# A convolution with a shorter transform: the filter's taps whose factor is exactly zero are left out

## Chip, cores, metric

One core of one Trainium2 chip. The metric is the device time of one execution in microseconds (us), here the median of three runs. Engines: TensorE (PE; PEld its weight loads), VectorE (DVE), ScalarE (ACT), GpSimd (POOL), and SyncE (SP), which only issues transfers.

## What is computed

Two parts, one behind the other, in float32. The first is a long convolution along the sequence; the second a layer of 2048 hidden units whose activation is a rational function.

```
x, v: (2, 12480, 128);  pos_emb: (12480, 64)
h_filt = (max(pos_emb @ w1, 0) @ w2) * exp(-0.01 * pos)[:, None]     # pos = 0 .. 12479, float32
L = 2 * 12480
y = irfft(rfft(x * v, L) * rfft(h_filt, L))[:, :12480, :]            # along the sequence
x2 = (x * y).reshape(24960, 128)
h = x2 @ w_in                                                        # 128 -> 2048
g = (a0 + a1 h + a2 h^2 + a3 h^3) / (1 + |b0| |h| + |b1| h^2 + 1e-6)
out = g @ w_out                                                      # 2048 -> 128
```

The factor exp(-0.01 pos) in float32 falls with the position and is exactly zero from position 10398 on.

## The kernel before

**The transform.** The sequence of length L = 24960 is cut as L = N1 * N2 with N2 = 128 and N1 = 195. A token is m * 128 + n2; there are M = 98 blocks m that hold tokens. The convolution of one channel has three steps. s1 multiplies, for each residue n2, the 98 blocks by a constant matrix f1 with K1 = 98 frequencies, cosine and sine side by side (2 * K1 = 196 columns), and turns the result by twiddle factors tw. s2 is a transform of 128 points over n2 (matrices dft), followed by the product with the filter's spectrum hg. s3 transforms back over the frequencies k2 (idft). The last step, over k1, is done for each residue in `attn_a` with constants g, a matrix of K1 x M for each.

**First part** (lines 243 to 615). The filter network (`hf_w`, `hf_t`, `hf_1`, `hf_2`) takes 16 groups of four residue pairs: positions are loaded with the blocks on the partitions (`load_pos`, L257, on SP's queue, three groups ahead, in a ring of three buffers), multiplied by the window on VectorE (L462, L466), transposed on TensorE (L481), and sent through two products (L488, L496), with copies on ScalarE between them (L484, L490, L502). Between these steps VectorE turns the weights of the second part from float64 words to float32 (`to_f32`, L312 to L328) and GpSimd makes the first products u = x * v (L230).

Then a loop over 32 groups of CG = 4 channels (L574) follows. In round g, in the order of the code: s1 of the filter for group g (`s1_mm`, then `s1h_out`: L160 and L161 with twh, and the four zh instructions L543 to L546 on VectorE), s2 of the filter for group g - 1 (L550, a copy hg on ScalarE, which is also stored to h_d), s1 of batch 0 (L142, L160 and L161 with tw on VectorE, zu on GpSimd, L166 and L167), s2 with the product for group g - 2 (L192 and L193 on VectorE, yy on GpSimd, L195 and L196), and s3 for group g - 3 (L557, two copies on ScalarE, L568 and L569 on GpSimd). A round ends with a piece of u on VectorE (L230) or, when these are done, a step of the weights. Each engine takes its instructions in the order in which they are written.

**Second part** (lines 621 to 1008). 52 tiles of up to five residues (490 tokens) are each taken in four steps of four blocks of hidden units. The order of a step is written out by hand in the loop at L987: ScalarE's L854 and L863 from PSUM, VectorE's L873, the first product h (L844 to L846) of the next step, and for earlier steps L891, L894, L887 on ScalarE, L899, L904, L908 on VectorE and the second product L922. Each step has three slots for one matrix product of another kind (`slot`, L950): the input of the next tile (`attn_a`, `attn_b`), or one step of the convolution of batch 1 for two channels (s1: L142, L154, L166, L167; s2: L177 to L180, L188, L195, L196; s3: L201, L202, L205). All of these share one PSUM buffer cv, so a slot's product starts when the one before has been read. After 64 groups of two channels the convolution is over and the tiles go on alone. All loads of this part, and the stores, are issued on SP's queue: x and v in pieces, hg from h_d, y in chunks of ten residues (yc, L753), g (L771).

Of the kernel before, what the change touches and what calls it, by code (L numbers as in the profile page):

```python
# [18 lines left out]
FO = 64  # L19
DFF = 2048  # L20
L = 2 * S
N2 = 128
N1 = L // N2
M = 98
K1 = 98
# [17 lines left out]
# slots of a tile that go to the next one: beside the convolution, and without it  # L43
# [3 lines left out]
def constants():  # L47
# [14 lines left out]
    # the filter's residues are taken in pairs n2 - 63.5 = +-(p + 1/2), as sums and differences  # L62
# [15 lines left out]
    pos = np.arange(S, dtype=np.float32)  # L78
    win = np.zeros((M * N2,), np.float32)
    win[:S] = np.exp(np.float32(-0.01) * pos)  # L80
    win = win.reshape(M, N2)
# [15 lines left out]
def build(ctx: ExitStack, tc, x, v, pos_emb, w1, w2, w_in, w_out, moe_a, moe_b,  # L97
# [16 lines left out]
    def rows(src, r0, n, t0, k, c0, c):  # L114
        """n blocks of k tokens, a block of N2 tokens apart, from token r0 * N2 + t0 of src (tokens, channels)"""
        w = src.shape[1]
        return bass.AP(src.tensor, src.offset + (r0 * N2 + t0) * w + c0, [[N2 * w, n], [w, k], [1, c]])

    def load_rows(dst, src, t0, k, c0, c, pad, queue=nc.sync):
        """tokens m * N2 + t0 ... of all m; the last m has half its tokens, and where it has none its place  # L120
        takes the tokens before (pad) or is left"""
# [17 lines left out]
    # steps of the convolution for n channels at a time: n / 2 banks  # L139
    def s1_mm(cvt, u, cl0, n):  # L140
        for c in range(n):
            nc.tensor.matmul(out=cvt[:, c // 2, c % 2 * 2 * K1:(c % 2 + 1) * 2 * K1],  # L142
                             lhsT=u[:, cl0 + c, :], rhs=f1, start=True, stop=True)

    def pair(pool):
        """room for both products of a pair of channels, in one"""
# [22 lines left out]
    def spectrum(cvt, n):  # L169
        """real and imaginary parts: a bank each, or both in one"""  # L170
# [62 lines left out]
    # weights of the second part, split into parts of 12 bits for the fast passes  # L233
# [9 lines left out]
    with ExitStack() as st:  # L243
# [4 lines left out]
        win, bdw1, bdw2 = flat[0][0:M, 0:N2], flat[1][:, 0:128], flat[2][:, 0:2 * D]  # L248
# [8 lines left out]
        def load_pos(p0):  # L257
            t = sp.tile([M, 2 * NPL, FO], F32, tag="wa", name="pos", bufs=3)
            load_rows(t[:, 0:NPL], pos_emb, H2 + p0, NPL, 0, FO, True)
            load_rows(t[:, NPL:], pos_emb, H2 - p0 - NPL, NPL, 0, FO, True)  # L260
# [31 lines left out]
        # weights and scalars of the second part  # L292
# [12 lines left out]
        def to_f32(raw, n):  # L305
            """float64 words (low, high) of n elements to float32: the high word gives sign,
            exponent and 20 bits of the fraction, the low word's upper 24 bits the rest."""
# [18 lines left out]
        def normal(fa, ie):  # L326
            """0 where the exponent is below float32's"""
# [712 lines left out]
```

## Time and profile before

| | us |
|---|---|
| median of 3 runs (2546.77 to 2547.78) | 2547.77 |
| profiled execution, span from first to last instruction | 2545.4 |
| VectorE busy | 2411.3 (95%) |
| TensorE busy | 2180.8 (86%) |
| ScalarE busy | 2103.6 (83%) |
| GpSimd busy | 561.5 (22%) |

The profile gives the span of its execution and no time around it. Busy times are those of instructions on the engine; a matmul's end is modelled, and an instruction that waits for a port while it runs counts as busy. Shares over the whole span mix stages with different limits, so the stages have to be read one by one. "L12" is line 12 of the kernel; "a <- b" are the names of the tiles written and read; "128x784" is partitions x elements.

### The profile page before, as it was taken

The page shows a single profiled execution, that of the slowest core. Times are in us where ns is not written, and L with a number is a line of the kernel's source. Part 1 is how long each engine was busy: PE and PEld are TensorE (multiplying, and loading weights), DVE is VectorE, ACT ScalarE, POOL GpSimd, SP SyncE. Part 2 cuts the span into 40 slices and gives each one's busy share as a digit, 9 for nine tenths or more (in the row PEclk, how much of TensorE's full clock was granted, in tenths as well). Part 3 has the DMA queues.
Part 4 walks back from the last instruction along what each step waited for, and adds up shares of the span by engine and source line. Part 5 has one row for each costly group of instructions (what it writes and reads, how often), then busy time and mean ns, then how long its engine had stood idle before and what let it go on. Part 6 is the DMA issues. An engine that isn't in the chain of part 4 may idle for free.

```text
span 2545.4 us, 33926 instructions
## 1 busy us (share of the span) xinstructions
PE 2180.8 (86%) x13344; PEld 1829.2 (72%) x13344; DVE 2411.3 (95%) x1945; ACT 2103.6 (83%) x1919; POOL 561.5 (22%) x522
## 2 busy tenths in 40 slices
PE   6888888789989998999899989888888898888877
PEld 4666665678877877788788767667776777776665
DVE  8999997799999998999899999999999999999997
ACT  6311121899999997999899999999999999999996
POOL 3466656222242224124321200000000000000000
PEclk9999989899999999999999999999999999999999
DMA  7444422822162235222322121111111111111100
GB/s 157 95 112 112 112 74 98 139 68 61 44 117 54 53 68 99 55 73 46 72 75 53 49 49 45 32 40 31 44 44 22 41 44 44 45 30 31 40 11 13
DMA packets 366001, 158.68 MB, mean 62 GB/s; under 512 B 299508, under 2 KB 347256, under 8 KB 362696
## 3 DMA queue, kind: packets, MB, share of 16 engines
q1 hardware_dynamic: 358696, 130.56, 23.2%
q10 hardware_dynamic: 7136, 25.86, 3.1%
q8 instruction: 107, 1.75, 0.3%
q14 instruction: 62, 0.51, 0.1%
HBM read 105.06 MB, written 51.31 MB: 61 GB/s over the span
## 4 chain that ended last, share of the span: by engine, by line
ACT 34%; DVE 30%; PE 21%; issue 9%; POOL 2%; DMA 1%; SPq 1%; ACTq 0%; DVEq 0%; POOLq 0%
ACT r L891 9%; ACT r L894 9%; ACT q L854 8%; PE acc L922 7%; DVE v L908 6%; ACT v L863 5%; DVE r L904 3%; DVE q L899 3%; PE cv L201 3%; PE cv L202 2%; DVE ta L188 2%; DVE v L873 2%; DVE tb L161 2%; PE cv L142 2%; DVE zh L544 2%
## 5 line engine op out<-in xcount | busy, mean ns | idle before, releaser
L922 PE MATMUL acc<-wout,v 128*128 128x128 f32 (+2 forms) x6656 | 833.2, 284 | 59.2 <-DVE v L908 35.2
L922 PEld LDWEIGHTS acc<-wout,v 128*128 128x128 f32 (+2 forms) x6656 | 790.6, 193 | 111.4 <-DVE v L908 55.3
L863 ACT ACTIVATE v<-h,sc 128x980 f32<-128x980 f32 (+1 forms) x416 | 683.2, 1642 | 8.0 <-PE acc L922 8.0
L854 ACT ACTIVATE q<-h 128x980 f32<-128x980 f32 (+1 forms) x416 | 613.7, 1559 | 6.4 <-PE h L846 6.4
L873 DVE SCALAR_TENSOR_TENSOR v<-v,sc,h 128x980 f32<-128x980 f32 (+1 forms) x416 | 504.9, 1214 | 59.7 <-ACT v L863 57.6
L887 ACT ACTIVATE q<-q,sc 128x1960 f32<-128x1960 f32 (+1 forms) x208 | 516.2, 2482 | 0.0
L891 ACT ACTIVATE r<-q,sc 128x1960 f32<-128x1960 f32 (+1 forms) x208 | 515.0, 2476 | 0.2 <-DVE v L908 0.2
L894 ACT ACTIVATE r<-r 128x1960 f32<-128x1960 f32 (+1 forms) x208 | 497.1, 2390 | 0.0
L899 DVE SCALAR_TENSOR_TENSOR q<-q,sc,r 128x1960 f32<-128x1960 f32 (+1 forms) x208 | 467.3, 2247 | 4.9 <-ACT r L894 1.1
L908 DVE SCALAR_TENSOR_TENSOR v<-v,sc,r 128x1960 f32<-128x1960 f32 (+1 forms) x208 | 465.5, 2238 | 0.1
L844 PE MATMUL h<-ahi,win_l 128*128 128x490 f32 (+1 forms) x832 | 365.0, 439 | 100.9 <-DVE v L873 98.5
L904 DVE SCALAR_TENSOR_TENSOR r<-q,r 128x1960 f32<-128x1960 f32 (+1 forms) x208 | 450.7, 2167 | 0.1
L845 PE MATMUL h<-alo,win_h 128*128 128x490 f32 (+1 forms) x832 | 320.6, 385 | 0.0
L846 PE MATMUL h<-ahi,win_h 128*128 128x490 f32 (+1 forms) x832 | 318.1, 382 | 0.0
L844 PEld LDWEIGHTS h<-ahi,win_l 128*128 128x128 f32 x832 | 158.5, 191 | 158.8 <-DVE v L873 133.3
L195 POOL TENSOR_TENSOR yy<-ta 128x196 f32<-128x196 f32 x64 | 122.1, 1908 | 368.3 <-DVE ta L188 368.3
L846 PEld LDWEIGHTS h<-ahi,win_h 128*128 128x128 f32 x832 | 158.7, 191 | 26.4
L845 PEld LDWEIGHTS h<-alo,win_h 128*128 128x128 f32 x832 | 159.4, 192 | 16.0 <-DVE alo L815 0.4
L790 PE MATMUL cv<-yc,gt 98*98 98x128 f32 x1004 | 130.9, 277 | 32.4 <-DVE an L796 29.9
L790 PEld LDWEIGHTS cv<-yc,gt 98*98 98x98 f32 x1004 | 115.0, 165 | 52.1 <-DVE an L796 48.6
L205 ACT ACTIVATE ys<-cv 98x512 f32<-98x512 f32 x64 | 76.9, 1202 | 76.2 <-PE cv L202 76.2
L201 PE MATMUL cv<-idft,yy 128*98 128x256 f32 x256 | 80.6, 396 | 57.3 <-DVE ta L188 33.1
(109 smaller groups left out, 2574.5 us busy)
## 6 DMA issues: line engine op xcount, KB each, us to landing
yc<-y_d SPq DMA_DIRECT2D x23, 980.0 KB
gt<-in_g_dram SPq DMA_DIRECT2D x48, 375.2 KB
h_d<-hg ACTq DMA_DIRECT2D x32, 392.0 KB
y_d<-ys ACTq DMA_DIRECT2D x16, 784.0 KB
hg<-h_d SPq DMA_DIRECT2D x64, 196.0 KB
y_d<-ys SPq DMA_DIRECT2D x16, 784.0 KB
xq<-in_x_dram SPq DMA_DIRECT2D x32, 196.0 KB
vq<-in_v_dram SPq DMA_DIRECT2D x32, 196.0 KB
```

Of the source, the lines that this page charges most:

```text
L844: nc.tensor.matmul(out=t[:, k, 0:w], lhsT=wl, rhs=hi[:, 0:w], start=True, stop=False)
L845: nc.tensor.matmul(out=t[:, k, 0:w], lhsT=wh, rhs=lo[:, 0:w], start=False, stop=False)
L854: nc.scalar.activation(out=halves(st_q[s], i, width(s)), in_=st_h[s, i], func=AF.Abs, **({} if short else {"scale": col("b0")}))
L863: nc.scalar.activation(out=v, in_=st_h[s, i], func=AF.Square, bias=col("s"))
L873: stt(out=v, in0=v, scalar=col("k"), in1=h, op0=ALU.add, op1=ALU.mult)
L887: nc.scalar.activation(out=whole(st_q, s), in_=whole(st_q, s), func=AF.Square, bias=col("dl"))
L891: nc.scalar.activation(out=whole(st_r, s), in_=whole(st_q, s), func=AF.Ln, **({"bias": col("ka")} if short else {}))
L894: nc.scalar.activation(out=whole(st_r, s), in_=whole(st_r, s), func=AF.Exp, scale=-1.0)
L899: nc.vector.scalar_tensor_tensor(out=q, in0=q, scalar=col("ka") if short else 0.0, in1=whole(st_r, s), op0=ALU.add, op1=ALU.mult)
L904: nc.vector.scalar_tensor_tensor(out=r, in0=whole(st_q, s), scalar=2.0, in1=r, op0=ALU.subtract, op1=ALU.mult)
L908: nc.vector.scalar_tensor_tensor(out=v, in0=v, scalar=col("p0" if short else "a0"), in1=whole(st_r, s), op0=ALU.add, op1=ALU.mult)
L922: nc.tensor.matmul(out=acc[j][0:k, q // 128, :], lhsT=g[:, i, q:q + k], rhs=wout[:, f, :], start=(f == 0 and q == 0), stop=(f == NF - 1), ...
```

## The change

The number of taps is counted when the program is built: TAPS is one more than the last position whose window factor is not zero. The filter network works on MF blocks (those that hold such taps) in place of all M. The length of the transform is the smallest odd number of blocks that holds S + TAPS - 1 tokens, N1 * 128, and K1 follows from it; all constants, tiles and instructions that are written in terms of K1, N1 or L take the new sizes. `s1_mm` takes the number of blocks that it sums over. The positions are loaded in two pieces of rows for each half, in place of 98 rows in one piece for the residues below 64, and 96 and 2 for the others; the window table has 96 rows in place of 98. Comments and docstrings are gone from the text, and the line numbers shift. The diff, without those:

```diff
@@ -18,11 +18,16 @@
 B, S, D = 2, 12480, 128
 FO = 64
 DFF = 2048
-L = 2 * S
 N2 = 128
-N1 = L // N2
 M = 98
-K1 = 98
+WINDOW = np.exp(np.float32(-0.01) * np.arange(S, dtype=np.float32))
+TAPS = int(np.flatnonzero(WINDOW)[-1]) + 1
+MF = min(M, -(-TAPS // N2))
+N1 = -(-(S + TAPS - 1) // N2) // 2 * 2 + 1
+L = N1 * N2
+K1 = (N1 + 1) // 2
 CG = 4
 NG = D // CG
 CY = 8
@@ -75,10 +80,9 @@
     ga = turn(k1[:, None, None] * (2 * N2 * m[None, None, :] + n2[None, :, None]), 2 * L)
     w = w[:, None, None]
     g = f(np.stack([np.cos(ga) * w, -np.sin(ga) * w * sg[None, :, None]], 2))
-    pos = np.arange(S, dtype=np.float32)
     win = np.zeros((M * N2,), np.float32)
-    win[:S] = np.exp(np.float32(-0.01) * pos)
-    win = win.reshape(M, N2)
+    win[:S] = WINDOW
+    win = win.reshape(M, N2)[:96]
     return {
         "f1": f1,
         "tw": tw,
@@ -136,14 +140,14 @@
     xb = [x[b] for b in range(B)]
     vb = [v[b] for b in range(B)]
 
-    def s1_mm(cvt, u, cl0, n):
+    def s1_mm(cvt, u, cl0, n, k=M):
         for c in range(n):
             nc.tensor.matmul(out=cvt[:, c // 2, c % 2 * 2 * K1:(c % 2 + 1) * 2 * K1],
-                             lhsT=u[:, cl0 + c, :], rhs=f1, start=True, stop=True)
+                             lhsT=u[0:k, cl0 + c, :], rhs=f1[0:k], start=True, stop=True)
 
     def pair(pool):
         t = pool.tile([N2, 2, 2, 2 * K1], F32, tag="ta", name="ta", bufs=2)
         return t, (t[:, 0], t[:, 1])
@@ -239,13 +243,13 @@
     y0 = wpool.tile([K1, NY, 2, NPT, CY], F32, name="y0")
     flag_i = wpool.tile([128, 1], I32, name="flag_i")
 
     with ExitStack() as st:
         sp = st.enter_context(tc.tile_pool(name="sp", bufs=1))
         spp = st.enter_context(tc.tile_pool(name="spp", bufs=4, space=PSUM))
 
         flat = [sp.tile([128, CG * 2 * K1], F32, tag=t, name=t + "0", bufs=2) for t in ("ta", "ta", "tb")]
-        win, bdw1, bdw2 = flat[0][0:M, 0:N2], flat[1][:, 0:128], flat[2][:, 0:2 * D]
+        win, bdw1, bdw2 = flat[0][0:96, 0:N2], flat[1][:, 0:128], flat[2][:, 0:2 * D]
         twh = sp.tile([N2, 2, 2 * K1], F32, name="twh")
         dfth = sp.tile([N2, 2, N2], F32, name="dfth")
         idfth = sp.tile([N2, 2, N2], F32, name="idfth")
@@ -256,8 +260,12 @@
 
         def load_pos(p0):
             t = sp.tile([M, 2 * NPL, FO], F32, tag="wa", name="pos", bufs=3)
-            load_rows(t[:, 0:NPL], pos_emb, H2 + p0, NPL, 0, FO, True)
-            load_rows(t[:, NPL:], pos_emb, H2 - p0 - NPL, NPL, 0, FO, True)
+            for o, t0 in ((0, H2 + p0), (NPL, H2 - p0 - NPL)):
+                if MF < M:
+                    for r0, r1 in ((0, MF // 16 * 16), (MF // 16 * 16, MF)):
+                        nc.sync.dma_start(out=t[r0:r1, o:o + NPL], in_=rows(pos_emb, r0, r1 - r0, t0, NPL, 0, FO))
+                else:
+                    load_rows(t[:, o:o + NPL], pos_emb, t0, NPL, 0, FO, True)
             pos_t[p0] = t
 
         load_pos(0)
@@ -450,20 +458,20 @@
                         raws.append(load_raw(src[k + 2], WN))
                 yield
 
         nb = H2 // NP
-        W = NP * M
+        W = NP * MF
         pT, rT = {}, {}
 
         def hf_w(p0):
             t = pos_t[p0]
-            pw = pos_t[p0] = sp.tile([M, NPL, 2, FO], F32, tag="wb", name="pw", bufs=2)
-            nc.vector.tensor_tensor(out=pw[:, :, 0], in0=t[:, 0:NPL],
-                                    in1=win[:, H2 + p0:H2 + p0 + NPL].unsqueeze(2).to_broadcast([M, NPL, FO]), op=ALU.mult)
+            pw = pos_t[p0] = sp.tile([MF, NPL, 2, FO], F32, tag="wb", name="pw", bufs=2)
+            nc.vector.tensor_tensor(out=pw[:, :, 0], in0=t[0:MF, 0:NPL],
+                                    in1=win[0:MF, H2 + p0:H2 + p0 + NPL].unsqueeze(2).to_broadcast([MF, NPL, FO]), op=ALU.mult)
             for i in range(NPL):
                 n2 = H2 - 1 - p0 - i
-                nc.vector.tensor_scalar(out=pw[:, i, 1], in0=t[:, 2 * NPL - 1 - i], scalar1=win[:, n2:n2 + 1],
+                nc.vector.tensor_scalar(out=pw[:, i, 1], in0=t[0:MF, 2 * NPL - 1 - i], scalar1=win[0:MF, n2:n2 + 1],
                                         scalar2=None, op0=ALU.mult)
 
         def hf_t(i):
@@ -478,8 +486,8 @@
             ps = cvs()
             for p in range(NP):
                 k = p0 - b0 + p
-                nc.tensor.transpose(out=ps[:, 0, p * M:(p + 1) * M], in_=pt[:, k].rearrange("m t c -> m (t c)"),
-                                    identity=ident[0:M, 0:M])
+                nc.tensor.transpose(out=ps[:, 0, p * MF:(p + 1) * MF], in_=pt[:, k].rearrange("m t c -> m (t c)"),
+                                    identity=ident[0:MF, 0:MF])
             pT[i] = ctile(sp, "zh", 2, CG).rearrange("p r c k -> p (r c k)")[:, 0:W]
             nc.scalar.activation(out=pT[i], in_=ps[:, 0, 0:W], func=AF.Identity)
@@ -493,11 +501,11 @@
             r = rT.pop(i)
             ps = cvs()
             for p in range(NP):
-                nc.tensor.matmul(out=ps[0:M, p // 2, (p % 2) * 2 * D:(p % 2 + 1) * 2 * D],
-                                 lhsT=r[:, p * M:(p + 1) * M], rhs=bdw2, start=True, stop=True)
-            src = ps[0:M].rearrange("m b (p s c) -> m (b p) s c", p=2, s=2)
+                nc.tensor.matmul(out=ps[0:MF, p // 2, (p % 2) * 2 * D:(p % 2 + 1) * 2 * D],
+                                 lhsT=r[:, p * MF:(p + 1) * MF], rhs=bdw2, start=True, stop=True)
+            src = ps[0:MF].rearrange("m b (p s c) -> m (b p) s c", p=2, s=2)
             for q in range(D // UQ):
-                o = hf[q].rearrange("m c (s p) -> m p s c", s=2)[:, i * NP:(i + 1) * NP]
+                o = hf[q][0:MF].rearrange("m c (s p) -> m p s c", s=2)[:, i * NP:(i + 1) * NP]
                 a = src[:, :, :, q * UQ:(q + 1) * UQ]
                 nc.scalar.activation(out=o, in_=a, func=AF.Identity)
@@ -576,7 +584,7 @@
             if a < NG:
                 zh[a] = ctile(sp, "zh", 2, CG)
                 t = cvs()
-                s1_mm(t, hf[a // gq], a % gq * CG, CG)
+                s1_mm(t, hf[a // gq], a % gq * CG, CG, MF)
                 s1h_out(t, zh[a])
             a = g - 1
             if 0 <= a < NG:
```

## Rows read from the trace of the kernel before

**Rows 1.** Stages: length, busy PE, PEld, DVE, ACT, POOL (instructions), clock, DMA share, GB/s.

```profile
0.00:83.00 83.00, 59.83 (x240) 39.31 (x240) 68.98 (x250) 53.58 (x127) 27.83 (x35) 0.96 0.65 147
83.00:430.00 347.00, 294.22 (x1376) 218.05 (x1376) 336.81 (x370) 64.59 (x111) 222.12 (x192) 0.95 0.38 97
430.00:500.00 70.00, 47.92 (x247) 40.26 (x246) 44.07 (x35) 50.63 (x45) 25.07 (x17) 0.80 0.86 161
500.00:1490.00 990.00, 901.89 (x5777) 782.98 (x5775) 934.31 (x642) 899.63 (x760) 286.45 (x279) 0.99 0.28 65
1490.00:2500.00 1010.00, 846.06 (x5508) 724.35 (x5509) 994.73 (x632) 1010.00 (x855) 0.00 (x0) 0.96 0.15 36
```

**Rows 2.** Timeline, one group of the loop: start, duration, engine, line, operation.

```profile
211.26 1.27 POOL L568 TENSOR_TENSOR ys<-qt 98x512 f32<-98x512 f32 x1
211.28 1.67 DVE L543 TENSOR_TENSOR zh<-ta,tb 64x392 f32<-64x392 f32 x1
...
215.73 0.97 DVE L160 TENSOR_TENSOR ta<-cs,tw 128x784 f32<-128x784 f32 x1
```

**Rows 3.** Timeline, a later group, and the first integer conversion of the loop.

```profile
338.32 1.10 DVE L312 TENSOR_SCALAR i<-raw 128x256 int32<-128x256 int32 x1
...
411.82 0.56 DVE L543 TENSOR_TENSOR zh<-ta,tb 64x392 f32<-64x392 f32 x1
...
416.11 0.97 DVE L160 TENSOR_TENSOR ta<-cs,tw 128x784 f32<-128x784 f32 x1
```

**Rows 4.** Chain of waits in order of time, the loop: start, duration, what.

```profile
115.87 1.54 DVE zh L544
...
331.67 1.53 DVE zh L544
```

**Rows 5.** What VectorE waited for, 500 to 1490: total us, times, longest.

```profile
DVE v L873 <- ACT v L863: 41.5, 63, 2.0
```

**Rows 6.** Timeline, one step beside the experts.

```profile
600.18 1.24 DVE L873 SCALAR_TENSOR_TENSOR v<-v,sc,h 128x980 f32<-128x980 f32 x1 [0.64 <-ACT v L863]
...
603.51 0.97 DVE L188 TENSOR_TENSOR ta<-cv,hg 128x784 f32<-128x784 f32 x1
...
604.53 0.67 PE L201 MATMUL cv<-idft,yy 128*98 128x256 f32 x2 [0.76 <-DVE ta L188]
...
609.82 0.97 DVE L154 TENSOR_TENSOR ta<-cv,tw 128x784 f32<-128x784 f32 x1
...
611.37 1.23 DVE L873 SCALAR_TENSOR_TENSOR v<-v,sc,h 128x980 f32<-128x980 f32 x1 [0.58 <-ACT v L863]
```

**Rows 7.** Groups by line and form: count, then busy us, mean ns.

```profile
L196 POOL TENSOR_TENSOR yy<-ta 128x196 f32<-128x196 f32 x64 | 38.9, 608 | 0.0
...
L196 POOL TENSOR_TENSOR yy<-pta,ptb 128x392 f32<-128x392 f32 x32 | 32.6, 1020 | 0.0
...
L796 DVE TENSOR_TENSOR an<-cv,xt 98x384 f32<-98x384 f32 x52 | 28.6, 550 | 8.4 <-PE cv L790 8.4
...
L796 DVE TENSOR_TENSOR an<-cv,xt 98x256 f32<-98x256 f32 x48 | 20.0, 417 | 3.3 <-PE cv L790 3.3
```

**Rows 8.** Timeline, SP's queue and VectorE in the filter network.

```profile
12.54 1.40 SPq L129 DMA_DIRECT2D pos<-in_pos_emb_dram  x1
...
14.30 0.32 SPq L127 DMA_DIRECT2D pos<-in_pos_emb_dram  x1
...
16.61 0.41 DVE L462 TENSOR_TENSOR pw<-pos,ta 98x256 f32<-98x256 f32 x1
```

**Rows 9.** What VectorE waited for, 0 to 90.

```profile
DVE pw L462 <- DMA ta<-in_win_dram: 4.4, 1, 4.4
...
DVE pw L466 <- DMA pos<-in_pos_emb_dram: 0.8, 1, 0.8
```

**Rows 10.** Chain of waits in order of time, the hand-over.

```profile
429.67 4.48 DMA y_d<-ys
...
484.18 9.54 DMA yc<-y_d
```


## Prediction

> **What bounds the kernel now.** I read the busy times by stage first [rows 1]. The filter network (0 to 83 us) has VectorE busy 69.0 of 83; the loop over channel groups, which makes the filter's spectrum and the convolution of batch 0, runs from 83 to about 430 with VectorE busy 336.8 of 347; then 70 us of hand-over at a DMA share of 0.86; then 990 us in which the experts run beside the convolution of batch 1 (VectorE 934, ScalarE 900, TensorE 902); then 1010 us of experts alone, where ScalarE is busy all the time. The last stage runs none of the changed steps except the weights of the inverse transform, so what is won must come from the others.
>
> In the loop the timeline of one group [rows 2] shows VectorE back to back, with L543 at 1.67 us. It begins 0.02 us behind GpSimd's L568 and ends 0.42 after it; the same form takes 0.56 where it comes ahead of that sum [rows 3]. L544 stands in the same way to GpSimd's next sum, L569, with 1.5 us [rows 4]. So the ends of these two are set by GpSimd's sums. L544 stands at 115.87 and, 20 groups later, at 331.67 [rows 4]: 10.79 us a group.
>
> Beside the experts the waits [rows 5] show 63 stalls of VectorE (41.5 us) for ScalarE's v, three a tile. The timeline of one step [rows 6] shows the ring behind them: L873 and L908, then L188 on VectorE, TensorE's four products L201/L202 that waited for L188, ScalarE's copy L205, its L854, L891 and L863, and then L873 again: 600.18 to 611.37, 11.19 us. L154 lies beside this ring, just before the stall of 0.58.
>
> **The change, part by part.** By the diff's own lines the window's last factor that is not zero is at 10397, so TAPS = 10398, MF = 82 blocks of 128 (before 98), N1 = 179 (195), K1 = 90 (98); the pieces of 80 and 2 rows agree with MF = 82. What scales is K1 along the free dimension: 784 elements become 720, 392 become 360, 196 become 180. What has M or K1 on the partitions (ys, attention, hf) keeps its free size, and such instructions I cost at nothing.
>
> *Prices of the shorter instructions* [rows 7]. VectorE: 384 to 256 elements is 550 to 417 ns, 1.04 ns an element; 64 elements less are 0.067 us, 32 less 0.033. GpSimd: yy at 392 and 196 elements takes 1020 and 608 ns, 2.1 ns an element, so 32 less are 0.067 us.
>
> *The loop.* Six PSUM products a group (L160, L161 twice each, L192, L193) give 6 x 0.067 = 0.40, four zh 4 x 0.033 = 0.13, together 0.53 us a group and 17.1 for 32 groups. The zh waits need a second look, since they end with GpSimd. L568 starts at 211.26 and L543 at 211.28. Both count from the u product before: VectorE through L160 and L161 (0.13 less), GpSimd through L195 and L196 (0.13 less). They move together, L568 keeps its 1.27 us, and the gain stays 0.53. Three groups run integer conversions beside GpSimd's yy (L312 takes 1.10 us in the first of them [rows 3]); GpSimd's 0.13 counts there too. Sum 17.5. TensorE (294 of 347 us busy, and its columns shrink too) and ScalarE (65) cover their own parts; should TensorE become late, its slack of some 53 us is the bound. The bounds of the loop: 21 us if VectorE now gets in front of L568 (0.16 a group more in 21 groups, from the 4.45 us that the four zh take, 211.28 to 215.73 [rows 2], against the 4.29 from 411.82 to 416.11, where L543 is free [rows 3]); 10.8 if GpSimd does not get cheaper with 360 elements, which leaves 0.34 a group, the four products ahead of u and the two zh at the end.
>
> *The filter network.* Transposes, the first product and two ScalarE copies fall from 392 columns to 328, all beside a busy VectorE; its own L462 and L466 keep 256 and 64 elements, so nothing is won there but a little of TensorE's time in the first groups. Each position load is four transfers in place of three, 16 loads: 16 more issues on SP's queue at 0.32 to 1.40 us [rows 8]. Behind them in that queue stand the window, the identity, raw weights, xq and vq, and for these wait L462, the transposes, the conversions and GpSimd's u products. The first L462 waits 4.4 us for the window [rows 9], now one issue later (+0.3). The load issued from 12.54 to 14.62 is used at 16.61, 2.0 us later [rows 8]; four loads lie before or at it, so +0.3 to +1.3. Once the integer conversions fill VectorE, SP has slack. I take +0.8 net, with 0 and +2 as ends.
>
> *The hand-over.* GpSimd's last four yy give 0.3. The store of ys (4.48 us on the chain) and the load of yc (9.54) [rows 10] lose 8% of their bytes: 0.36 and 0.76. Sum 1.4; bounds 0 (the x and v loads, which don't shrink, set the pace) and 4.
>
> Here a page bears on it. The rows show two transfers of 98 partitions and their times, not over how many engines they ran. The Trainium skill, page "DMA: Bandwidth & Descriptors", section on why a DMA increments its semaphore by 16, says that a transfer takes the largest number of engines up to 16 that divides the outer dimension of both sides: 98 rows would run on 14, 90 on 15, 82 on 2, 80 on 16. By that rule (an estimate) an engine's share of yc falls by 14% in place of 8%, and the sum gains another 0.9 us. No row here shows the number of engines.
>
> *Beside the experts.* L188 and L154 fall by 0.067 each, 64 times. L188 is in the ring and counts: 64 x 0.067 = 4.3. L154 lies before the stall and only widens it; the experts' own instructions hide it. If the ring were not what ends the step, both would count, 8.6; if loads and GpSimd's u products set this stage, 0. I take 4.3, because the 63 stalls are nearly as many as the 64 groups. No wait is added here.
>
> *Sum.* -17.5 + 0.8 - 1.4 - 4.3 = -22.4 us against the profiled execution, whose span is 2545.4. What lies around the span isn't shown; the runs shown (median 2547.8) are 2.4 above it, and I keep that: 2525.4, rounded to 2525.
>
> **The rivals.**
>
> *A: the order at VectorE and GpSimd turns.* The margin between L568 and L543 is 0.02 us. If VectorE gets in front, the loop gives 21 and not 17.5; with the hand-over at its larger bound it is 2519, with both products beside the experts counted 2515. For it: so thin a margin. Against: both sides shorten by the same 0.13.
>
> *B: GpSimd or the loads swallow part.* GpSimd's instructions cost nearly the same for 360 as for 392 elements: loop 10.8, time about 2532; with nothing beside the experts 2536. For it: GpSimd's part of the loop is on the path in every group [rows 2]. Against: its price by size [rows 7].
>
> *C: no change worth telling.* A measurement of this kernel tells 0.2%, about 5 us, from none. The parts outside the loop give 4.9 together, so the loop must give nothing: another resource must take over at once at 10.8 us a group. TensorE's 294 of 347 us [rows 1], or 9.2 for each of 32 groups, is the nearest; it would have to shrink by nothing and wait more. 2543.
>
> *D: the position loads pace the filter network, and the kernel is slower.* The added transfer of two rows lands last, behind x and v at a DMA share of 0.65 in this stage [rows 1], and VectorE waits for it in every load: 16 x 2.0 us (from the last issue to the use, 14.62 to 16.61 [rows 8]) = 32, less the 23.2 of the other parts = 9 slower, 2557. It decides from 23.2 / 16 = 1.45 us a load. Against: half the loads had such a two-row transfer before, and positions were waited for once, 0.8 us [rows 9]. The Trainium skill, same page, section "Rules for kernel authors", speaks for it: many small transfers should be coalesced, since under 64 KB one pays mostly overhead. An added transfer here has 2 KB; by the rule it is nearly all overhead, which costs time only where someone waits for it.
>
> That the change doesn't shorten anything is excluded by the piece sizes; the shapes in its trace will say so.
>
> **How the numbers follow.** Forecast 0.60 (its own range 2520 to 2530), A 0.17, B 0.15, C 0.05, D 0.03. Below 2514 only all larger bounds together lead, above 2534 the worst of B, C and D; that leaves about 0.13 out. Faster by over 0.2%: 0.60 + 0.17 + 0.15 = 0.92; within 0.2% 0.05; slower 0.03.
>
> **What would show it.** L160 to L193 at about 0.90 us with 720 elements; the loop's L544 every 10.2 to 10.3 us; L543 still near 1.6 (or 0.5, which is A); yy at 0.95 in GpSimd's free groups (B: 1.02); L873 to L873 around the ring at 11.12, with the stall widened from 0.58 to about 0.65; the first group at most 2 us later than now; the experts alone unchanged in length. A loop period above 10.5, or L462 waiting for pos again and again, would make the prediction wrong.

## The result, and the profile after

The changed kernel takes 2523.56 us (median of four runs, 2522.18 to 2524.88) against 2547.27 us before (four runs beside them, 2545.42 to 2547.78): a ratio of 0.9904, 95% interval 0.989 to 0.9918, or 23.7 us. Forecast were 2525 us. The profiled execution has a span of 2521.5 us against 2545.4, 23.9 less.

Cut at four instructions that both kernels have, the 23.9 us lie here (us; the first product with twh opens the loop, the last product with tw closes it, the first product with hg beside the experts ends the hand-over, the last ys copy ends the convolution):

| stretch | before | after | difference | forecast |
|---|---|---|---|---|
| start to the first product with twh | 82.80 | 84.42 | +1.6 | +0.8 |
| the loop, to its last product with tw | 337.08 | 320.46 | -16.6 | -17.5 |
| hand-over, to the first product with hg | 81.76 | 80.28 | -1.5 | -1.4 |
| beside the experts, to the last ys copy | 979.40 | 971.79 | -7.6 | -4.3 |
| the experts alone, to the end | 1064.4 | 1064.6 | +0.2 | 0 |

The stages of the changed kernel, in the columns of [rows 1] and cut where each stage now lies:

```profile
0.00:84.00 84.00, 60.86 (x240) 38.97 (x240) 68.84 (x248) 52.53 (x127) 28.10 (x34) 0.92 0.64 138
84.00:415.00 331.00, 284.87 (x1376) 219.36 (x1376) 321.36 (x371) 62.79 (x112) 213.57 (x193) 0.92 0.40 97
415.00:484.00 69.00, 52.01 (x249) 42.94 (x250) 44.15 (x34) 51.28 (x46) 24.43 (x17) 0.75 0.82 155
484.00:1466.00 982.00, 886.74 (x5773) 765.03 (x5771) 924.00 (x642) 897.71 (x759) 278.60 (x279) 0.99 0.28 62
1466.00:2476.00 1010.00, 846.51 (x5506) 724.68 (x5507) 995.07 (x632) 1010.00 (x855) 0.00 (x0) 0.96 0.16 35
```

VectorE still has hardly a gap in the loop (321 of 331 us). The timeline of one group shows the pair of [rows 2] again, L576 for L568 and L551 for L543:

```profile
206.47 1.26 POOL L576 TENSOR_TENSOR ys<-qt 90x512 f32<-90x512 f32 x1
206.49 1.62 DVE L551 TENSOR_TENSOR zh<-ta,tb 64x360 f32<-64x360 f32 x1
...
210.78 0.91 DVE L164 TENSOR_TENSOR ta<-cs,tw 128x720 f32<-128x720 f32 x1
...
216.76 1.26 POOL L576 TENSOR_TENSOR ys<-qt 90x512 f32<-90x512 f32 x1
216.79 1.63 DVE L551 TENSOR_TENSOR zh<-ta,tb 64x360 f32<-64x360 f32 x1
```

VectorE is again 0.02 us behind GpSimd's sum, and its zh ends 0.38 behind that sum's end (0.42 before). The chain of waits gives the period: L552 answers to L544 in [rows 4], and here 16 groups lie between the two.

```profile
136.25 1.50 DVE zh L552
...
300.61 1.50 DVE zh L552
```

164.36 / 16 = 10.27 us a group (10.79 before). The prices of the shorter instructions, from the groups by line and form (count, busy us, mean ns):

```profile
L158 DVE TENSOR_TENSOR ta<-cv,tw 128x720 f32<-128x720 f32 x64 | 57.7, 902 | 5.7 <-PE cv L146 5.7
...
L200 POOL TENSOR_TENSOR yy<-ta 128x180 f32<-128x180 f32 x64 | 36.6, 572 | 0.0
L200 POOL TENSOR_TENSOR yy<-pta,ptb 128x360 f32<-128x360 f32 x32 | 30.9, 966 | 0.0
```

902 ns for 720 elements, where 0.90 us was forecast, and 966 ns for GpSimd's 360 (0.95 forecast, 1020 before). Beside the experts the ring of [rows 6] reads so, with L881 for L873, L192 for L188, L205 for L201 and L158 for L154:

```profile
583.12 1.24 DVE L881 SCALAR_TENSOR_TENSOR v<-v,sc,h 128x980 f32<-128x980 f32 x1 [0.68 <-ACT v L871]
...
586.44 0.90 DVE L192 TENSOR_TENSOR ta<-cv,hg 128x720 f32<-128x720 f32 x1
...
587.40 0.67 PE L205 MATMUL cv<-idft,yy 128*90 128x256 f32 x2 [0.84 <-DVE ta L192]
...
592.68 0.90 DVE L158 TENSOR_TENSOR ta<-cv,tw 128x720 f32<-128x720 f32 x1
...
594.22 1.23 DVE L881 SCALAR_TENSOR_TENSOR v<-v,sc,h 128x980 f32<-128x980 f32 x1 [0.63 <-ACT v L871]
```

From L881 to L881 it is 11.10 us (11.19 before, 11.12 forecast), and the stall behind L158 is 0.63 (0.58 before, 0.65 forecast). The waits of VectorE in the stage, answering to [rows 5]:

```profile
DVE v L881 <- ACT v L871: 45.6, 63, 1.5
DVE ta L158 <- PE cv L146: 5.7, 2, 2.9
```

The same 63 stalls, longer by 4.1 us together: that is where L158's 64 x 0.067 went. The second row, two waits of VectorE for the first product of a new quarter of channels, comes back below.

### The profile page after: what moved, and what is told of

It reads as the page before. It is cut to its first block, busy times and chain, and to the rows that moved or that the text cites. A ratio compares the mean times of both kernels' runs of the same rounds, so it can differ in the third digit from the quotient of the medians.

```text
span 2521.5 us, 33957 instructions
## 1 busy us (share of the span) xinstructions
PE 2163.8 (86%) x13344; PEld 1817.2 (72%) x13344; DVE 2385.3 (95%) x1945; ACT 2099.0 (83%) x1919; POOL 544.7 (22%) x522
## 4 chain that ended last, share of the span: by engine, by line
ACT 35%; DVE 28%; PE 24%; issue 9%; POOL 2%; DMA 1%; SPq 0%; ACTq 0%; DVEq 0%; POOLq 0%
ACT r L902 9%; ACT r L899 9%; ACT q L862 7%; PE acc L930 7%; DVE v L916 7%; ACT v L871 6%; DVE r L912 4%; DVE q L907 3%; PE cv L205 3%; PE cv L206 2%; ACT q L895 2%; DVE ta L192 2%; DVE v L881 2%; PE cs L146 1%; PE cv L146 1%
## 5 line engine op out<-in xcount | busy, mean ns | idle before, releaser
L871 ACT ACTIVATE v<-h,sc 128x980 f32<-128x980 f32 (+1 forms) x416 | 640.2, 1539 | 5.5 <-PE acc L930 5.5
L862 ACT ACTIVATE q<-h 128x980 f32<-128x980 f32 (+1 forms) x416 | 582.2, 1458 | 6.6 <-PE h L854 6.6
L881 DVE SCALAR_TENSOR_TENSOR v<-v,sc,h 128x980 f32<-128x980 f32 (+1 forms) x416 | 505.3, 1215 | 64.1 <-ACT v L871 62.3
L895 ACT ACTIVATE q<-q,sc 128x1960 f32<-128x1960 f32 (+1 forms) x208 | 495.6, 2383 | 0.0
L899 ACT ACTIVATE r<-q,sc 128x1960 f32<-128x1960 f32 (+1 forms) x208 | 494.7, 2378 | 0.2 <-DVE v L916 0.2
L902 ACT ACTIVATE r<-r 128x1960 f32<-128x1960 f32 (+1 forms) x208 | 476.5, 2291 | 0.0
L907 DVE SCALAR_TENSOR_TENSOR q<-q,sc,r 128x1960 f32<-128x1960 f32 (+1 forms) x208 | 466.3, 2242 | 4.9 <-ACT r L902 1.1
L199 POOL TENSOR_TENSOR yy<-ta 128x180 f32<-128x180 f32 x64 | 117.8, 1841 | 367.5 <-DVE ta L192 367.5
L798 PE MATMUL cv<-yc,gt 90*98 90x128 f32 x1004 | 130.8, 277 | 33.4 <-DVE an L804 30.7
L798 PEld LDWEIGHTS cv<-yc,gt 90*98 90x98 f32 x1004 | 114.8, 165 | 53.5 <-DVE an L804 49.7
L209 ACT ACTIVATE ys<-cv 90x512 f32<-90x512 f32 x64 | 76.9, 1202 | 71.3 <-PE cv L206 71.3
L205 PE MATMUL cv<-idft,yy 128*90 128x256 f32 x256 | 79.9, 394 | 61.4 <-DVE ta L192 36.5
```

The source lines that it names most:

```text
L862: nc.scalar.activation(out=halves(st_q[s], i, width(s)), in_=st_h[s, i], func=AF.Abs, **({} if short else {"scale": col("b0")}))
L871: nc.scalar.activation(out=v, in_=st_h[s, i], func=AF.Square, bias=col("s"))
L881: stt(out=v, in0=v, scalar=col("k"), in1=h, op0=ALU.add, op1=ALU.mult)
L895: nc.scalar.activation(out=whole(st_q, s), in_=whole(st_q, s), func=AF.Square, bias=col("dl"))
L899: nc.scalar.activation(out=whole(st_r, s), in_=whole(st_q, s), func=AF.Ln, **({"bias": col("ka")} if short else {}))
L902: nc.scalar.activation(out=whole(st_r, s), in_=whole(st_r, s), func=AF.Exp, scale=-1.0)
```

## The experiments

Each kernel is the changed kernel with one edit, the last with two of them; times are medians beside runs of the kernel before on the same chip, and periods, entries and steps are read from the profiled execution.

### Which half of the change does it

**The filter network alone.** The taps are left out there, with its position loads in four transfers; the transform keeps its length.

```diff
-N1 = -(-(S + TAPS - 1) // N2) // 2 * 2 + 1
+N1 = 2 * S // N2
```

> The taps are left out in the filter network alone (82 blocks, positions in pieces of 80 and 2 rows); the transform keeps its length of 195 blocks and K1 = 98. Theory (the gain comes from K1 along the free dimension, and the position loads cost): the first twh product at 84.4 us as in the changed kernel (before 82.8), everything behind as before, so 1 to 2 us slower than before, 2549. Rival (the smaller filter network brings part of the gain): 3 us or more faster than before, loop entered before 82.

Measured: 2547.85 us, ratio 1.000 (0.999 to 1.001). The loop is entered at 82.78 us, as before and not at the 84.4 that was expected, though VectorE now waits longer for positions (before, once, 0.8 us [rows 9]):

```profile
DVE pw L470 <- DMA pos<-in_pos_emb_dram: 2.0, 2, 1.6
```

The extra transfers do cost a wait, and the entry is not later for it: other small waits of the first 30 us came out shorter (ScalarE's for the scalars 2.9 in place of 3.9).

**The transform alone.** The filter network keeps 98 blocks and its old transfers.

```diff
-MF = min(M, -(-TAPS // N2))
+MF = M
...
-    win = win.reshape(M, N2)[:96]
+    win = win.reshape(M, N2)
...
```

> The transform is short (K1 = 90), the filter network works on all 98 blocks with its three transfers for each load of positions. Theory: loop entered at 82.8 us, loop period 10.25 us, beside the experts as in the changed kernel: 1.6 us faster than the changed kernel, 2522. Rival (fewer blocks matter): slower than the changed kernel by 3 or more, 2527.

Measured: 2523.0 us, ratio 0.9906 (0.989 to 0.9923): the whole gain. And the loop is entered at 84.04 us, late, with the old three transfers, where 82.8 was expected. So the late entry does not belong to the transfers, against the working of the forecast.

**Positions in one transfer of 96 rows a half.**

```diff
-                if MF < M:
-                    for r0, r1 in ((0, MF // 16 * 16), (MF // 16 * 16, MF)):
-                        nc.sync.dma_start(out=t[r0:r1, o:o + NPL], in_=rows(pos_emb, r0, r1 - r0, t0, NPL, 0, FO))
-                else:
-                    load_rows(t[:, o:o + NPL], pos_emb, t0, NPL, 0, FO, True)
+                nc.sync.dma_start(out=t[0:96, o:o + NPL], in_=rows(pos_emb, 0, 96, t0, NPL, 0, FO))
```

> The changed kernel with each half of the positions in one transfer of 96 rows: two transfers for each load in place of four. Theory (SP's issues in the first 25 us make the filter network late): positions are not waited for at 17 us, loop entered at 81 to 83 us in place of 84.4, 1.5 to 3 us faster than the changed kernel, 2521. Rival (what lands late is set by the bytes at the DMA engines, and 96 rows have more of them than 82): loop entered at 84 or later, no gain.

Measured: 2522.85 us (0.9902, 0.9885 to 0.9918), entry 84.09. Two transfers or four, the entry stays late and the time the same.

### What is on the path in the loop

**GpSimd's first yy of a group in two halves.**

```diff
-        nc.gpsimd.tensor_tensor(out=yv[:, 0], in0=ta[:, 0, :], in1=tb[:, 1, :], op=ALU.subtract)
+        w = n * K1
+        for o in range(0, w, w // 2 if n == CG else w):
+            k = slice(o, o + (w // 2 if n == CG else w))
+            nc.gpsimd.tensor_tensor(out=yv[:, 0, k], in0=ta[:, 0, k], in1=tb[:, 1, k], op=ALU.subtract)
```

> The changed kernel with GpSimd's first yy of a loop group cut into two halves; by its rows at 180 and 360 elements this adds 2 x 0.57 - 0.97 = 0.18 us to GpSimd between the u product and the ys sums, and nothing to VectorE. Theory (the end of the zh instructions is set by GpSimd, so GpSimd's time behind u is on the path): loop period 10.25 + 0.18 = 10.43, 4 to 6 us slower than the changed kernel. Rival (VectorE's own instructions add up to the period): 10.25, no change; or VectorE gets in front of the first ys sum, L551 at 0.53, and the period falls to 10.1.

Measured: 2520.06 us (0.9894, 0.9877 to 0.991), 3.5 us below the changed kernel; the period is 10.15. The theory's longer group did not come; its other clause did. The timeline (first zh now L554, first ys sum L579):

```profile
205.94 0.55 DVE L554 TENSOR_TENSOR zh<-ta,tb 64x360 f32<-64x360 f32 x1
206.06 1.55 POOL L579 TENSOR_TENSOR ys<-qt 90x512 f32<-90x512 f32 x1
...
216.11 0.55 DVE L554 TENSOR_TENSOR zh<-ta,tb 64x360 f32<-64x360 f32 x1
```

VectorE is in front, its first zh takes 0.55 in place of 1.62 us, and GpSimd's sum takes 1.55 in place of 1.26. This is rival A of the prediction, made by an edit: it is worth 0.12 us a group, and the loop takes 318.2 us in place of 320.5. Only these 2.3 us belong to the edit. Of the 3.2 by which the span is shorter, 0.6 is lost at the entry (85.03 us) and 1.9 lies in the experts alone, which the edit does not touch and which took 1062.7 to 1065.4 us over the fourteen kernels.

**GpSimd's first zu (ahead of u) in two halves.**

```diff
-        nc.gpsimd.tensor_tensor(out=z[:, 0], in0=a[:, :, 0:K1], in1=bb[:, :, K1:], op=ALU.add)
+        for o in range(0, n, 2):
+            c = slice(o, o + 2)
+            nc.gpsimd.tensor_tensor(out=z[:, 0, c], in0=a[:, c, 0:K1], in1=bb[:, c, K1:], op=ALU.add)
```

> The changed kernel with GpSimd's first zu of a group cut into two halves: 2 x 0.54 - 0.83 = 0.25 us more of GpSimd in each loop group, ahead of the u product. Theory (GpSimd waits for u there, with some 0.7 us of slack): loop period 10.25, no change beyond 1 us. Rival (GpSimd is on the path in the whole group): period 10.5, 5 to 8 us slower.

Measured: 2527.33 us (0.992, 0.9903 to 0.9936), period 10.42. The timeline:

```profile
214.18 0.97 POOL L172 TENSOR_TENSOR zu<-ta,tb 128x180 f32<-128x180 f32 x2 [3.43 <-DVE tb L165]
...
215.11 0.83 POOL L173 TENSOR_TENSOR zu<-ta,tb 128x360 f32<-128x360 f32 x1
...
215.56 1.30 DVE L236 TENSOR_TENSOR hu<-xq,vq 97x512 f32<-97x512 f32 x1
```

The two halves take 0.97 us (0.83 for the whole), and the period is 0.15 longer: all of it counts. VectorE's u product (L236) begins while GpSimd's second zu (L173) still runs, takes 1.30 us where it took 1.15, and ends 0.92 us behind that zu. The theory's slack of 0.7 us does not exist.

**VectorE's second product with twh in two halves.** It lies behind u, beside GpSimd's yy.

```diff
-        nc.vector.tensor_tensor(out=tb, in0=src, in1=tw[:, 1:2, :].unsqueeze(1).to_broadcast(sh), op=ALU.mult)
+        for o in range(0, n // 2, 1 if cut else n // 2):
+            c = slice(o, o + (1 if cut else n // 2))
+            nc.vector.tensor_tensor(out=tb[:, c], in0=src[:, c], in1=tw[:, 1:2, :].unsqueeze(1).to_broadcast(
+                [N2, c.stop - c.start, 2, 2 * K1]), op=ALU.mult)
...
-        a, bb = s1_twiddle(sp, cvt, twh, CG)
+        a, bb = s1_twiddle(sp, cvt, twh, CG, True)
```

> The changed kernel with the second twh product (the one just ahead of L551) cut into two halves: 0.07 to 0.13 us more of VectorE between u and zh in each group. Theory (behind u the path runs through GpSimd's yy and ys, and VectorE only waits longer or shorter): L551 gets shorter by what the cut costs, period 10.25 in the groups with u, time unchanged within 1.5 us. Rival (VectorE's instructions add up): period 10.32 to 10.38, 2 to 4 us slower.

Measured: 2523.29 us (0.9908, 0.9892 to 0.9925), period 10.27.

```profile
206.69 1.26 POOL L579 TENSOR_TENSOR ys<-qt 90x512 f32<-90x512 f32 x1
206.77 1.57 DVE L554 TENSOR_TENSOR zh<-ta,tb 64x360 f32<-64x360 f32 x1
```

The zh behind it starts 0.08 us after GpSimd's sum and takes 1.57 in place of 1.62: hidden, as the theory had it.

**VectorE's second product with tw in two halves.** The same edit of the function, called for the product ahead of u.

```diff
-        a, bb = s1_twiddle(pool, cvt, tw, n)
+        a, bb = s1_twiddle(pool, cvt, tw, n, n == CG)
```

> In the loop, VectorE's second product with tw (ahead of the u product, 0.90 us) is cut into two halves, which costs VectorE about 0.08 us more (the same cut of a product beside the experts, in the ring, cost 0.08 a group). Theory: ahead of u VectorE and GpSimd are both on the path; VectorE's part counts at least half: the period goes from 10.27 to 10.31 to 10.36, the loop is 1.3 to 2.7 us longer, span near 2523.5. Rival: GpSimd alone sets the time ahead of u (its own cut cost 0.13 of 0.25), and VectorE's longer part is hidden: period 10.27, last product at 404.9, span 2521.5.

```profile
212.40 0.96 DVE L167 TENSOR_TENSOR tb<-cs,tw 128x360 f32<-128x360 f32 x2
```

Measured: 2523.52 us (0.9909, 0.9893 to 0.9926), too little to tell in the time; but the product takes 0.96 in place of 0.90 us, the period is 10.34 in place of 10.27, and the loop ends at 406.9 (404.9). All of the 0.06 counts. The changed kernel's rows show how both can count whole:

```profile
213.24 0.90 DVE L197 TENSOR_TENSOR ptb<-cs,hg 128x720 f32<-128x720 f32 x1
213.45 0.83 POOL L171 TENSOR_TENSOR zu<-ta,tb 128x360 f32<-128x360 f32 x1
...
214.05 1.15 DVE L234 TENSOR_TENSOR hu<-xq,vq 97x512 f32<-97x512 f32 x1
```

GpSimd's zu starts when VectorE's second product with tw is done, and u ends 0.92 us behind the second zu. In the 20 groups with u between 120 and 320 us it ends 0.89 to 0.93 us behind it, in the changed kernel and with zu, tw, twh or yy cut alike. So the path of a group runs through VectorE's two products with tw, GpSimd's zu, then u, and behind u through GpSimd's sums, as long as they come first. VectorE's two products with hg run beside zu and end 0.14 us ahead of it; no run cut one of them, but by these rows they are hidden.

### What is on the path beside the experts

**The product with tw in two halves** (L158).

```diff
-            nc.vector.tensor_tensor(out=t, in0=src.unsqueeze(1).to_broadcast(t.shape),
-                                    in1=tw.unsqueeze(2).to_broadcast(t.shape), op=ALU.mult)
+            for r in range(2):
+                nc.vector.tensor_tensor(out=t[:, r], in0=src, in1=tw[:, r:r + 1].to_broadcast([N2, 2, 2 * K1]), op=ALU.mult)
```

> The changed kernel with the tw product beside the experts (L158) issued as two halves, which adds one VectorE instruction, 0.07 to 0.13 us from start to start, 64 times. Theory (it lies beside the ring, ahead of VectorE's stall for ScalarE's v): the stall of 0.62 shrinks to about 0.5, ring 11.10 as before, time unchanged within 1 us. Rival (VectorE is the bound there, and both products count): 4.5 to 8 us slower.

Measured: 2519.0 us (0.9892, 0.9875 to 0.9908). The timeline:

```profile
592.80 0.96 DVE L159 TENSOR_TENSOR ta<-cv,tw 128x360 f32<-128x360 f32 x2
...
594.33 1.24 DVE L881 SCALAR_TENSOR_TENSOR v<-v,sc,h 128x980 f32<-128x980 f32 x1 [0.57 <-ACT v L871]
```

The cut costs VectorE 0.06 us, the stall behind it pays, and the step stays: hidden, as forecast. That the kernel came out 3.1 us shorter in span was in neither expectation. Of this 1.7 us lie ahead of the last ys copy, and the rest in the experts alone. The 1.7 come from two groups: one at the half, 1.3 us longer, and one that is 3.1 shorter. Where a quarter of the channels is used up (near 1200 us), GpSimd has to finish u for the next one first. In the changed kernel TensorE and VectorE wait for that:

```profile
1183.34 14.14 POOL L234 TENSOR_TENSOR uq<-xq,vq 98x512 f32<-98x512 f32 x5
...
1197.53 1.57 PE L146 MATMUL cv<-f,uq 98*128 98x180 f32 x4 [3.66 <-POOL uq L234]
...
1199.21 0.91 DVE L158 TENSOR_TENSOR ta<-cv,tw 128x720 f32<-128x720 f32 x1 [2.87 <-PE cv L146]
```

That group, from one product with hg to the next, takes 20.57 us before, 19.47 after and 16.32 here, without VectorE's wait. What turned is again the order of two engines. A piece of u on GpSimd takes 1.3 us, or 3.2 where a VectorE instruction comes first. In the changed kernel VectorE's L907 goes ahead of the seventh piece, which takes 3.25; here the piece goes ahead (1.27), and L907 waits:

```profile
1190.40 2.69 DVE L907 SCALAR_TENSOR_TENSOR q<-q,sc,r 128x1960 f32<-128x1960 f32 x1
...
1191.73 3.92 DVE L907 SCALAR_TENSOR_TENSOR q<-q,sc,r 128x1960 f32<-128x1960 f32 x1
```

The first row is the changed kernel's, the second this one's.

**The product with hg in two halves** (L192).

```diff
-                                    in1=h.unsqueeze(2).to_broadcast(t.shape), op=ALU.mult)
+            for r in range(2):
+                nc.vector.tensor_tensor(out=t[:, r], in0=src, in1=h[:, r:r + 1].to_broadcast([N2, 2, 2 * K1]), op=ALU.mult)
```

> The changed kernel with the hg product beside the experts (L192) issued as two halves, again 0.07 to 0.13 us 64 times. Theory (it is in the ring, TensorE waits for it): ring 11.10 + 0.07 to 0.13, 4.5 to 8 us slower than the changed kernel, 2528 to 2532. Rival (ScalarE or TensorE sets the step and VectorE has slack): unchanged.

```profile
587.19 0.97 DVE L193 TENSOR_TENSOR ta<-cv,hg 128x360 f32<-128x360 f32 x2
...
588.31 0.64 PE L205 MATMUL cv<-idft,yy 128*90 128x256 f32 x2 [1.02 <-DVE ta L193]
```

Measured: 2525.86 us (0.9921, 0.9905 to 0.9938), 2.3 us above the changed kernel and so short of the 4.5 expected. TensorE's wait for it grows from 0.84 to 1.02, the step from 11.10 to 11.23, and the last ys copy is 3.8 us later, although this kernel lost the wait of the quarter's change too (16.26). The three kinds of ordinary group (about 11.1, 15.1 and 17.3 us) take 0.11 us more on average; 62 times that, less the 3.2 of the wait, make up nearly all of the 3.8. So the product with hg is in the ring, and the one with tw is not.

### Where the late entry and the hand-over come from

Every tile that has K1 in its size lies before others in memory, so the change moves the tiles that are loaded, too. **Room for 98 frequencies** puts the first part's tiles, and nearly all of the second's, back to their old places.

```diff
-    f1 = const.tile([M, 2 * K1], F32, name="f1")
-    tw = const.tile([N2, 2, 2 * K1], F32, name="tw")
+    f1 = const.tile([M, 2 * 98], F32, name="f1")[:, 0:2 * K1]
+    tw = const.tile([N2, 4 * 98], F32, name="tw")[:, 0:4 * K1].rearrange("p (a b) -> p a b", a=2)
...
-        flat = [sp.tile([128, CG * 2 * K1], F32, tag=t, name=t + "0", bufs=2) for t in ("ta", "ta", "tb")]
+        flat = [sp.tile([128, CG * 2 * 98], F32, tag=t, name=t + "0", bufs=2) for t in ("ta", "ta", "tb")]
...
```

> The changed kernel with the constants, twiddle products and their sums placed in memory with room for 98 frequencies, so that everything else lies where it lay in the kernel before; no instruction changes its size. It asks where the later loop entry comes from (82.8 before and with the filter network alone changed, 84.0 to 84.5 in every kernel with the short transform, with three or four position transfers). Theory: the place in memory of the tiles that the first loads fill sets how long these loads take; with the old places the fourth position load lands in time and the loop begins at 82.8 to 83.2, 1.2 to 1.6 us earlier, the rest as before, span near 2520. Rival: it is not the places but the order in which the engines and transfers happen to meet; the loop begins at 84.4 again, span near 2521.5.

Measured: 2523.02 us (0.9909, 0.9892 to 0.9925), entry 83.26, near the theory, though the span is 2521.3. (The range of entries in the expectation misses one kernel: with GpSimd's first yy in halves it is 85.03.) What had not been looked for came with it: the hand-over is back at 81.77 us. Issuing the 32 transfers of x and v for batch 1 takes from 429.94 to 465.58, 35.6 us (first and last of them, on SP's queue):

```profile
429.94 0.41 SPq L131 DMA_DIRECT2D xq<-in_x_dram  x1
...
464.32 1.26 SPq L131 DMA_DIRECT2D vq<-in_v_dram  x1
...
467.75 0.90 SPq L761 DMA_DIRECT2D yc<-y_d  x1
```

In the changed kernel the same 32 take 32.2:

```profile
430.90 0.41 SPq L131 DMA_DIRECT2D xq<-in_x_dram  x1
...
462.18 0.96 SPq L131 DMA_DIRECT2D vq<-in_v_dram  x1
...
465.13 0.90 SPq L761 DMA_DIRECT2D yc<-y_d  x1
```

The three kernels with the old places have 35.3 to 35.6 us and a hand-over of 81.7 to 81.8; the ten with the new ones 31.2 to 32.2 and 80.1 to 80.9. **64 unused bytes** in front of all tiles test the alignment alone.

```diff
+    const.tile([128, 16], F32, name="room")
     f1 = const.tile([M, 2 * K1], F32, name="f1")
```

> The changed kernel with one unused tile of 64 bytes a partition at the start of memory: everything behind it lies 64 bytes higher, and no instruction or transfer changes. It tells whether it is the alignment of the tiles that are loaded. By the program's own addresses the tiles for positions, x, v and raw weights of the first part begin on a multiple of 128 bytes in the kernel before and in the one with room for 98 frequencies (loop entered at 82.8 and 83.3), and 64 bytes off one in the changed kernel (84.4); the tiles for x and v of batch 1 are the other way round (32 loads issued in 35.3 to 35.6 us there, in 31.2 to 32.2 in the ten kernels with the new places). 64 bytes turn both round again, at places that are in neither kernel. Theory (alignment): the loop is entered at 83.0 to 83.6, the 32 loads of x and v for batch 1 take 35 to 36 us, the hand-over from the loop's last product to the first product with hg takes 81.5 to 82, and the two cancel: span 2521 to 2522. Rival (it is other properties of the old places, as banks or distance): 64 bytes change nothing, entry 84.4, loads 31.2 to 32.2 us, span 2521.5; or one of the two turns and the other does not.

Measured: 2525.48 us (2522.87 to 2531.6; 0.9901, 0.9885 to 0.9918). For batch 1 the theory held: 35.4 us.

```profile
432.47 0.41 SPq L132 DMA_DIRECT2D xq<-in_x_dram  x1
...
466.47 1.40 SPq L132 DMA_DIRECT2D vq<-in_v_dram  x1
```

For the entry neither expectation holds: it is at 85.94. ScalarE waited 4.7 us here for two small loads of scalars; but it waited 3.9 in the kernel before, which enters at 82.80, and 2.9 in the changed one, so this wait alone does not explain it. The execution is also 5 us or more above the other three of this kernel, and its hand-over of 83.8 is longer than either theory had it. How late a kernel enters is settled by about 30 us: the last scalar step on VectorE (`flag_i`) starts at 30.20 before, 31.61 in the changed kernel, 30.49 with room for 98 and 33.17 here, and from there to the entry all four take 52.6 to 52.8 us.

The traces say more of the loads themselves. Their 128-byte packets, the rows of x and v, take 13.0 ns on average in the first part (5 to 83 us) in the four kernels whose tiles there lie on a multiple of 128 bytes, this one among them, and 13.3 to 13.8 in the ten others. During the 32 loads it is the other way round: 14.8 to 15.4 ns in the four, 13.0 in the ten. So the packets go with the alignment in both places; that the entry's 1.6 us come from it is not shown.

### Both splits that gained, in one kernel

The edit to GpSimd's first yy and the edit to the product with tw beside the experts, as above:

```diff
+            nc.gpsimd.tensor_tensor(out=yv[:, 0, k], in0=ta[:, 0, k], in1=tb[:, 1, k], op=ALU.subtract)
...
+                nc.vector.tensor_tensor(out=t[:, r], in0=src, in1=tw[:, r:r + 1].to_broadcast([N2, 2, 2 * K1]), op=ALU.mult)
```

> The two splits that came out below the changed kernel, in one kernel: GpSimd's first yy sum of a loop group in two halves (it puts VectorE ahead of the first ys sum) and the tw product beside the experts in two halves. They lie in different stages. Theory: the gains add up. The loop runs at 10.14 us a group and ends near 403.2 (changed kernel 404.9), the ring stays at 11.14, and the tail keeps what the second split won; span 2521.5 - 3.2 - 3.1 = 2515, time about 2516.5. Rival: what the second split won (1.7 us ahead of the last ys copy, 1.3 behind it) is a matter of where the transfers happened to fall and does not come again with another loop; then the time is that of the first split alone, about 2520.

Measured: 2518.77 us (2517.73 to 2520.49; 0.9893, 0.9877 to 0.991), the lowest median of all; period 10.15, the quarter's change at 16.33, span 2515.9. The rival is out: the gain at the quarter came again. In the spans the gains add up, 5.6 of 6.3 us; in the times the kernel is 4.8 below the changed one and can't be told from either split alone.

## Why the prediction was right, step by step

**The loop** (forecast -17.5, measured -16.6). The size is right: 0.52 us a group was won where 0.53 was worked out; 32 x 0.52 = 16.6. The path is right in part. The products with tw count whole (0.06 of 0.06), and behind u GpSimd's yy and ys lead, of which the forecast had shortened yy by as much as VectorE's part. But it counted VectorE's two products with hg (0.13), which by the rows end ahead of GpSimd's zu, and left out zu, which counts whole. Each zu fell from 0.88 to 0.82 us, two of them by 0.12: the term that was left out is as large as the one that was counted without need, and that is luck. The 0.02 us by which L551 comes late is the margin on which rival A stands. The change left the order as it was, because both sides got shorter by the same; the edit to yy turned it.

**The filter network** (+0.8, measured +1.6). The size lies within the bounds that were given, the cause does not. It was put down to the fourth transfer of each position load. The filter network alone has that transfer and its wait, and enters on time; the transform alone has three transfers and enters late. Room for 98 frequencies takes 1.2 of the 1.6 away, so the places of the tiles are the best reading, and the packets of x and v are indeed slower there. But one profiled execution stands behind each number, the kernel with 64 bytes entered late, and how much is alignment stays open.

**The hand-over** (-1.4, measured -1.5). Right in size by the wrong reason. The store of ys fell from 4.48 [rows 10] to 4.36 us only, in the changed kernel's chain:

```profile
414.28 4.36 DMA y_d<-ys
```

The load of yc, 900 KB in place of 980, still took 9.87 us, against 9.54, in the chain of the kernel with room for 98 frequencies; in the changed kernel it is not on the chain.

```profile
467.75 9.87 DMA yc<-y_d
```

So neither 8% less came about, nor the 14% less worked out from the rule of the Trainium skill (page "DMA: Bandwidth & Descriptors", on why a DMA increments its semaphore by 16): no run here bears the rule out. What shortened the hand-over is that the loads of x and v were issued in 3.2 us less at their new places; 1.5 of it reached the first product, because VectorE's work for the experts then ended last.

The Trainium skill, page "DMA: Bandwidth & Descriptors", section "How a descriptor splits into AXI transactions", says that a descriptor which does not start on a multiple of 256 bytes begins at the multiple below it and pays for that part. A row of x or v here has 128 bytes; with a tile 64 bytes off, every second row crosses such a multiple. The 35.4 us against 31.2 to 32.2 agree in direction, on the side that is written, which the section does not treat.

**Beside the experts** (-4.3, measured -7.6). The step is right: L192 is in the ring, L158 is not, as the two splits show. The size of a group is nearly right: the 51 ordinary groups gained 0.074 us on average where 0.067 was put, which makes 4.7 for 64. The other 2.9 came mostly where groups wait for a new quarter of x and v: 1.0 in the group that waits for u near 1200 us and 0.9 in five groups around the half, over what these would have gained anyhow; 0.6 lie behind the last product with hg. The forecast had counted those waits as fixed. They hang on which of GpSimd's pieces of u VectorE holds up, as the split of L158 showed by taking 3.1 us off one of them.

**The rivals.** A did not come by itself; made by an edit, it gave 2.3 us in the loop, where 3.5 was put. B: GpSimd's 360 elements cost 966 ns, not 1020, so it fell. C and D fell with the time. The errors of the terms cancelled to some extent (+0.8, +0.9, -0.1, -3.3, and +0.2 in the experts alone); that 2525 lay 1.4 us from the result is better than the terms were.

## What to carry to other kernels

When instructions of two engines slow each other, see which of them starts first and by how much: here 0.02 us decides over 0.12 us a group, and an edit that makes GpSimd a little later made the loop 2.3 us shorter. To learn whether an instruction is on the path, split it into two halves (0.06 to 0.14 us here) and read the period, not the total: the total moved by 3 us for reasons that lie in a single group and in a stage that no edit touches. A change of sizes moves every tile behind; compare addresses before giving a gain or a loss in loads to the bytes.

## What was not expected of the hardware

The same 32 loads took 31.2 to 32.2 us to issue into tiles on a multiple of 128 bytes and 35.3 to 35.6 into tiles 64 bytes off, in fourteen kernels without an exception; their 128-byte packets took 13.0 ns on average in the first case and 14.8 to 15.4 in the second. A VectorE instruction of 360 elements on 64 partitions takes 0.55 us when it starts ahead of a GpSimd sum, and the sum 1.55; when it starts 0.02 us behind the sum it takes 1.62, and the sum 1.26. Whichever comes second pays.
